# One list-scheduled order for attention and its filler products, with a shared pool of PSUM banks

## The chip, the core and the metric

The kernel runs on one core of one Trainium2 chip. The metric is the device time of one execution, in microseconds (us). The engines are TensorE (PE, matrix products), VectorE (DVE), ScalarE (ACT), GpSimd (POOL) and SyncE (SP, which issues the DMAs here).

## What is computed

```python
def _A_ref(x, wqkv, wo):                 # 32 heads of 16, 2048 tokens, D = 512
    q, k, v = split_heads(x @ wqkv)
    p = softmax((q @ k.T) * 16 ** -0.5)
    return merge_heads(p @ v) @ wo
def _B_ref(x, w_gate, w_up, w_down):     # F = 1792
    return ((x @ w_gate) * (x @ w_up)) @ w_down
xn = layernorm(x)
out = x + _A_ref(xn) * silu(_B_ref(xn))
```

All of it is float32. Products that need the accuracy are made as three products of high and low parts (`hi*hi + hi*lo + lo*hi`, each part in the float32r type).

## The kernel before

**Start.** `early` normalises the tokens, transposes them, and makes V and the first projections. It has PSUM banks of its own. It also makes the first 21 (`LEAD`) rounds of scores.

**Attention.** Work is cut into 32 units: 8 groups of four heads by 4 chunks of 512 queries. A unit has 16 key tiles of 128 keys. Each key tile takes, for each of the four heads `j`:

- a score `s` (`score`, L545, product at L550): queries by keys, from which DVE takes the maximum (L552). It runs 21 rounds ahead of where its unit is used. `maxima` (L554) gathers these, negates them and sends them through DRAM into extra rows of the query tile.
- a transposed score `t` (`expo`, L571, product at L575): keys by queries, with the negated maximum folded in by those extra rows. ACT takes the exponential (L577) into a tile `e`, of which there are 12.
- a V product (`pv`, L580, product at L586): V of the key tile, 32 columns a head, by `e`. The four heads stand side by side in the columns of the array and in one PSUM bank, summed over the 16 key tiles.

Heads with even `j` use the lower 64 rows of the array, odd ones the upper 64. So `t` of one head and `s` of another (`j ^ 1`) run at the same time, one on each half.

**Filler.** Everything else that PE has to do runs between these: projections of Q and K for later heads, then the gated product (gate `g`, up `u`, down `y`), then the output product (`z`). These sums are made in pairs of outputs by `pair` (L230): the sum of an output is split into the lower and the upper 64 rows of the operands. In the first half of a pair, output 0 takes its lower rows (L243) while output 1 takes its upper rows (L247); then the two change sides. Between the halves ACT reads one element of output 1 (`look`, L251), so that the second half waits until the first is in PSUM.

**Order.** The order of PE, ACT and DVE is the order in which the program issues instructions. The loop at L781 goes through 512 rounds, one key tile each: `t`, `s`, `t`, `s`, then a fixed share of the filler (`Filler.part`, 4 to 6 slots of two products), then `t`, `s`, `t`, `s`, then the V product of the round before. Copies and other work on ACT and DVE are put off by a fixed number of steps (`soon`, L99). PSUM's eight banks are divided by kind: two for `t`, three for `s`, one for `pv`, two for the filler (`BUFS`, L41). After the last round `finish` (L589) and `last_heads` (L503) close the last unit, and the last four heads are added to the last chunk of the output (`final`).

Of the kernel before, what the change touches and what calls it, by code (L numbers as in the profile page):

```python
# [32 lines left out]
FFN_ROUNDS = 484  # L33
SLOTS = 24 * (NC * (NG // 2 - 1) + 1) + 36 * NF * NC
SPLIT_ROUNDS = 4
EBUFS = 12
HBUFS = 2
FINAL_AT = 8
# [8 lines left out]
def body(ctx, tc, x, wqkv, wo, wg, wu, wd, out):  # L47
# [48 lines left out]

    steps, waiting = [0], []

    def soon(n, fn):  # L99

        if n:
            waiting.append((steps[0] + n, fn))
            waiting.sort(key=lambda w: w[0])
        else:
            fn()

    def flush():
        while waiting:
            waiting.pop(0)[1]()

    def step():
        steps[0] += 1
        while waiting and waiting[0][0] <= steps[0]:
            waiting.pop(0)[1]()

# [114 lines left out]
    def pair(outs, banks, sums, more=((), ()), stop=True):  # L230

        for k in range(2):
            low, high = [*more[k], *sums[k]], sums[1 - k]
            yield k, len(low)
            if k == 0:
                outs += [psum(tag, name) for tag, name in banks]
            for n in range(len(low)):  # L240
                m = n - len(low) + len(high)
                l, r = low[n]
                nc.tensor.matmul(outs[k], l[LOWER], r[LOWER], start=k == 0 and n == 0,  # L243
                                      stop=(stop or k == 0) and n == len(low) - 1, skip_group_check=k == 1)
                if m >= 0:
                    l, r = high[m]
                    nc.tensor.matmul(outs[1 - k], l[UPPER], r[UPPER], start=k == 0 and m == 0,  # L247
                                          stop=(stop or k == 0) and m == len(high) - 1, skip_group_check=k == 1)
                yield 1
            if k == 0:  # L250
                nc.scalar.activation(look, outs[1][0:1, 0:1], AF.Copy)  # L251


# [16 lines left out]

    def proj_pair(m, which):

        outs = []
        yield from pair(outs, [("misc", f"p{w}_{m}_{c}") for _, w, c in which],
                        [terms(lambda d: ws[0][:, d], lambda d: ws[1][:, d],
                               lambda d: xh[c][:, d], lambda d: xl[c][:, d], ND) for ws, _, c in which])
        raws = [qp.tile([P, D], F32, name="qr", bufs=3) for _ in outs]
        fst["high"] = nc.scalar.activation(raws[0], outs[0], AF.Copy)
        nc.vector.tensor_copy(raws[1], outs[1])
        for o, (_, w, c) in zip(raws, which):  # L280
            hl = qp.tile([P, 2, D], F32R, name="hl", bufs=HBUFS)
            split_rows(o, hl[:, 0], hl[:, 1])
            qk_store(hl, m, w, c)
# [19 lines left out]
    later = []  # L303

# [4 lines left out]
    def silu(fp, c, y):  # L309
        for t in range(4):  # L310
            e = fp.tile([P, D], F32, name="e2", bufs=1)
            nc.scalar.activation(e, y[:, t], AF.Tanh, scale=0.5)
            nc.gpsimd.tensor_scalar(e, e, 0.5, 0.5, op0=OP.mult, op1=OP.add)
            nc.gpsimd.tensor_tensor(y[:, t], e, y[:, t], op=OP.mult)
            if c < NC - 1:
                dma(YD[c][:, t], y[:, t])
            yield

    def gu_weights(f):
        fs = slice(f * P, (f + 1) * P)  # L320
        return [split(n, w[:, fs]) for n, w in (("w1", wg), ("w0", wu))]

    def ffn(nxt):
        fp = fst["fp"]
        for c in range(NC):
            if c == 0:
                fh, fl = xh[0], xl[0]
            else:
                fh, fl = [keep.tile([P, ND, 512], F32R, name=n) for n in ("fh", "fl")]
                dmar(fh, XD[c][0])  # L330
                dmar(fl, XD[c][1])
            y = fp.tile([P, 4, D], F32, name="y")
            for ti, fs in enumerate(THIRDS):
                hh = fp.tile([P, 5, 512], F32R, name="hh")
                hl = fp.tile([P, 5, 512], F32R, name="hl")
                dh = fp.tile([P, 5, D], F32R, name="dh")
                dl = fp.tile([P, 5, D], F32R, name="dl")
                for i, f in enumerate(fs):
                    ws = nxt
                    if not (c == NC - 1 and f == NF - 1):  # L340
                        nxt = gu_weights((f + 1) % NF)
                    outs = []
                    yield from pair(outs, [("misc", f"{n}{c}_{f}") for n in "gu"], [terms(lambda d: wh[:, d], lambda d: wl[:, d],
                                                 lambda d: fh[:, d], lambda d: fl[:, d], ND) for wh, wl in ws])
                    g = fp.tile([P, 512], F32, name="g", bufs=1)
                    nc.scalar.activation(g, outs[0], AF.Copy)
                    h = fp.tile([P, 512], F32, name="h", bufs=1)
                    soon(1, lambda h=h, u=outs[1], g=g: nc.vector.tensor_tensor(h, u, g, op=OP.mult))
                    soon(4, lambda h=h, hi=hh[:, i], lo=hl[:, i]: hidden(h, hi, lo))
                    raw = fp.tile([P, D], F32, name="wdr", bufs=2)  # L350
                    dma(raw, wd[f * P:(f + 1) * P])
                    nc.gpsimd.tensor_copy(dh[:, i], raw)  # L352
                    nc.gpsimd.tensor_tensor(dl[:, i], raw, dh[:, i], op=OP.subtract)
                if c == NC - 1 and fs[-1] == NF - 1:
                    fst["y"] = y
                    fst["w"] = [keep.tile([P, ND, D], F32R, name=n) for n in ("fh", "fl")]
# [4 lines left out]
                for t in range(0, 4, 2):  # L361
                    outs = []
                    yield from pair(outs, [("misc", f"y{c}_{ti}_{u}") for u in (t, t + 1)], [terms(lambda i: hh[:, i, u * P:(u + 1) * P],
                                                 lambda i: hl[:, i, u * P:(u + 1) * P],
                                                 lambda i: dh[:, i], lambda i: dl[:, i], len(fs)) for u in (t, t + 1)])
                    for n, o in enumerate(outs):
                        def add(o=o, y=y[:, t + n], first=ti == 0, n=n):
                            if first and n:
                                nc.vector.tensor_copy(y, o)
                            elif first:  # L370
                                nc.scalar.activation(y, o, AF.Copy)
                            else:
                                nc.vector.tensor_tensor(y, o, y, op=OP.add)
                        soon(n if ti else 0, add)
            later.append(silu(fp, c, y))

    ops = {}

    def o_split(c, tiles):
# [9 lines left out]
        ops[c] = now[0], tiles  # L391
# [5 lines left out]
    def prepare():  # L397

        done = [(NG - 1) * NC + c in finished for c in range(NC)]
        if 0 not in ops:  # L400
            if done[0] and "w" in fst:
                o_split(0, small_tiles())
        for c in (1, 2):
            if c not in ops and done[c] and ("big", c) in fst:
                h, l = fst["big", c]
                o_split(c, [(h[:, d], l[:, d]) for d in range(ND)])
        if 3 not in ops and "first" in fst:
            o_split(3, small_tiles())
# [18 lines left out]
    def ending():  # L427

# [6 lines left out]
        side = [big(n).bitcast(F32) for n in ("hh", "dl")]  # L435
        fst["big", 1] = big("hl"), big("dh")

        def until(c):
            while c not in ops or now[0] < ops[c][0] + SPLIT_ROUNDS:
                yield  # L440

        def chunk(c):
            yield from until(c)
            for t in range(0, 4, 2):
                here = side[t // 2]
                got = [(here[:, n], here[:, 2 + n]) for n in range(2)]

                def loads(t=t, here=here):
                    dma(here[:, 0:2], YD[c][:, t:t + 2])
                    dma(here[:, 2:4], x[(4 * c + t) * P:(4 * c + t + 2) * P].rearrange("(t p) d -> p t d", p=P))  # L450
                soon(2, loads)
                outs = []
                yield from pair(outs, [("misc", f"z{c}_{u}") for u in (t, t + 1)], [o_terms(c, u) for u in (t, t + 1)])
# [384 lines left out]
```

## Time and profile before

| | |
|---|---|
| median of 3 runs | 1816.97 us (1816.04 to 1818.2) |
| profiled execution, span from first to last instruction | 1815.7 us |
| PE busy | 1794.1 us (99%) |
| DVE busy | 1474.4 us (81%) |
| ACT busy | 1238.3 us (68%) |
| POOL busy | 580.7 us (32%) |
| DMA | 145.72 MB, mean 80 GB/s |
| mean granted clock of TensorE | 0.995 |

In a row of the profile, `L575 PE MATMUL t<-qs,ks` is an instruction of line 575 on PE that writes tile `t` and reads `qs` and `ks`; `x8` after it is the number of instructions merged into the row, and what stands in brackets is idle time of the engine before it and what ended it. Busy time of PE is the union of overlapping matmuls, whose ends are modelled: a busy PE is not yet a PE at its best rate. Better to read are the starts of its instructions.

### The profile page before, as it was taken

Reading aid. Unit: us, or ns where it says so; the run is one execution under the profiler, and the core shown is the slowest. Engines: PE = TensorE matmul, PEld = TensorE weight load, DVE = VectorE, ACT = ScalarE, POOL = GpSimd, SP = SyncE. Lnnn points to the kernel's source line nnn. Section 1 sums busy time; section 2 is a strip of 40 time slices with the busy share of each in tenths; the row PEclk is TensorE's granted clock in tenths of the full one; section 3 lists DMA queues with packets and bytes.
Section 4 is the critical chain, followed back from the end, with each engine's and each line's share of the span. In section 5 each row is a group of like instructions: output and inputs, shape, how many; then the busy total and the mean of one; then the engine's idle time right before and its main releaser. Section 6 shows DMA issues by size and latency. Waiting matters only on the chain.

```text
span 1815.7 us, 34194 instructions
## 1 busy us (share of the span) xinstructions
PE 1794.1 (99%) x13568; PEld 991.1 (55%) x13568; DVE 1474.4 (81%) x2456; ACT 1238.3 (68%) x2365; POOL 580.7 (32%) x647
## 2 busy tenths in 40 slices
PE   8899999999999999999999999999999999999998
PEld 5565555555555555555555555555555555555555
DVE  8488888888888888888888888888888888888832
ACT  5137676777776767777777777776767767767674
POOL 5321332431331325232132441431315323223441
PEclk9899999999999999999999999999999999999999
DMA  5424633520222122321115220411125111111352
GB/s 198 112 54 163 225 118 115 148 62 22 68 64 54 49 86 80 80 55 42 39 42 131 69 63 22 94 52 33 52 79 126 46 40 57 34 48 45 110 156 79
DMA packets 117227, 145.72 MB, mean 80 GB/s; under 512 B 12620, under 2 KB 74060, under 8 KB 114380
## 3 DMA queue, kind: packets, MB, share of 16 engines
q1 hardware_dynamic: 117068, 143.55, 27.7%
q8 instruction: 106, 1.74, 0.4%
q14 instruction: 53, 0.43, 0.1%
HBM read 95.94 MB, written 47.45 MB: 79 GB/s over the span
## 4 chain that ended last, share of the span: by engine, by line
PE 94%; DVE 2%; DMA 2%; POOL 1%; issue 0%; ACT 0%; SPq 0%; POOLq 0%; ACTq 0%; DVEq 0%
PE pv L586 27%; PE t L575 21%; PE s L550 11%; PE y L243 6%; PE u L243 5%; PE g L243 4%; PE u L247 4%; PE g L247 4%; PE y L247 3%; PE p L243 3%; PE v L224 2%; PE p L247 2%; PE z L243 1%; PE z L247 1%; DMA wdr<-in_wd_dram 1%; PE p L224 0%
## 5 line engine op out<-in xcount | busy, mean ns | idle before, releaser
L552 DVE TENSOR_REDUCE mx<-s 128x1 f32<-128x512 f32 x2048 | 1311.7, 683 | 268.5 <-PE s L550 162.7
L577 ACT ACTIVATE e<-t 128x512 f32<-128x512 f32 x2048 | 1111.9, 596 | 427.0 <-PE s L550 236.3
L550 PE MATMUL s<-ks,qs 48*128 48x512 f32 x2048 | 700.1, 427 | 10.0 <-DMA ks<-KD 8.8
L575 PE MATMUL t<-qs,ks 50*128 50x512 f32 x2048 | 705.2, 426 | 0.3 <-ACT e L577 0.3
L575 PEld LDWEIGHTS t<-qs,ks 50*128 50x128 f32 x2048 | 347.2, 185 | 499.4 <-ACT e L577 474.0
L586 PE MATMUL pv<-e,V 128*32 128x512 f32 x4096 | 545.7, 605 | 0.0
L550 PEld LDWEIGHTS s<-ks,qs 48*128 48x128 f32 x2048 | 337.4, 185 | 33.9 <-issue 12.9
L138 POOL CAST w0h<-w0r 128x512 fp32r<-128x512 f32 x60 | 36.7, 612 | 407.2 <-PE u L243 257.9
L586 PEld LDWEIGHTS pv<-e,V 128*32 128x32 f32 x4096 | 81.0, 108 | 156.5 <-issue 147.3
L352 POOL CAST dh<-wdr 128x512 fp32r<-128x512 f32 x56 | 33.8, 614 | 182.9 <-PE y L247 92.4
L247 PE MATMUL u<-fh,w0h 64*128 64x512 f32 x224 | 88.2, 394 | 0.1
L247 PE MATMUL y<-dh,hh 64*128 64x512 f32 x224 | 88.1, 393 | 0.0
L243 PE MATMUL u<-fh,w0l 64*128 64x512 f32 x224 | 88.0, 393 | 0.0
L243 PE MATMUL g<-fh,w1l 64*128 64x512 f32 x224 | 87.8, 392 | 0.0
L247 PE MATMUL g<-fl,w1h 64*128 64x512 f32 x224 | 87.8, 392 | 0.0
L243 PE MATMUL u<-fh,w0h 64*128 64x512 f32 x224 | 87.7, 392 | 0.0
L247 PE MATMUL g<-fh,w1h 64*128 64x512 f32 x224 | 87.7, 392 | 0.0
L243 PE MATMUL g<-fh,w1h 64*128 64x512 f32 x224 | 87.7, 391 | 0.0
L243 PE MATMUL u<-fl,w0h 64*128 64x512 f32 x224 | 87.6, 391 | 0.0
L243 PE MATMUL g<-fl,w1h 64*128 64x512 f32 x224 | 87.6, 391 | 0.0
L243 PE MATMUL y<-dh,hh 64*128 64x512 f32 x224 | 87.6, 391 | 0.0
L243 PE MATMUL y<-dl,hh 64*128 64x512 f32 x224 | 87.5, 391 | 0.0
(250 smaller groups left out, 2885.1 us busy)
## 6 DMA issues: line engine op xcount, KB each, us to landing
w1r<-in_wg_dram SPq DMA_DIRECT2D x56, 256.0 KB
w0r<-in_wu_dram SPq DMA_DIRECT2D x56, 256.0 KB
wdr<-in_wd_dram SPq DMA_DIRECT2D x56, 256.0 KB
qs<-QD SPq DMA_DIRECT2D x64, 192.0 KB
ks<-KD SPq DMA_DIRECT2D x12, 768.0 KB
KD<-hl SPq DMA_DIRECT2D x16, 512.0 KB
QD<-hl SPq DMA_DIRECT2D x16, 512.0 KB
OD<-tr SPq DMA_DIRECT2D x31, 256.0 KB
```

The source lines that it names most:

```text
L138: cast = nc.gpsimd.tensor_copy(hi, raw)
L224: nc.tensor.matmul(o, l(d), r(d), start=k == d == 0, stop=k == 2 and d == ND - 1)
L243: nc.tensor.matmul(outs[k], l[LOWER], r[LOWER], start=k == 0 and n == 0, stop=(stop or k == 0) and n == len(low) - 1, skip_group_check=k == 1)
L247: nc.tensor.matmul(outs[1 - k], l[UPPER], r[UPPER], start=k == 0 and m == 0, stop=(stop or k == 0) and m == len(high) - 1, skip_group_chec ...
L352: nc.gpsimd.tensor_copy(dh[:, i], raw)
L550: nc.tensor.matmul(o, QS[i][b:b + KB, pr, t * P:(t + 1) * P], k[b:b + KB, pr, kc * 512:(kc + 1) * 512], start=True, stop=True)
L552: nc.vector.tensor_reduce(MX[i][:, j, t, kc:kc + 1], o, axis=AX.X, op=OP.max)
L575: nc.tensor.matmul(o, k[b:b + KR, pr, kt * P:(kt + 1) * P], QS[i][b:b + KR, pr], start=True, stop=True)
L577: nc.scalar.activation(e, o, AF.Exp, scale=DH ** -0.5)
L586: nc.tensor.matmul(fst["pv"][32 * j:32 * j + 32], V[:, kt, h0:h0 + 32], es[j], start=kt == 0, stop=kt == NT - 1)
```

## The change

The loop of rounds, `Filler`, `pair`, `soon` and the steps go away. A list scheduler (`Order`) writes out the order of PE, ACT and DVE while the program is built. It keeps a clock for each of the three engines, with fixed costs of each kind of work as constants, and at each step picks what goes next on the two row halves.

- **Banks.** Seven PSUM banks form one pool that `t`, `s` and the filler share; one bank is left for `pv`. A bank comes free at a time that the scheduler works out.
- **Two rolling streams.** The filler is a sequence of single outputs (`Out`). Each has a lower part, made on the lower rows, then a look, then an upper part on the upper rows. The lower part of the next output and the upper part of the one before run at the same time, and a slot may also hold `t` or `s` beside a product of the filler. At most two outputs are held (`HELD`), a third if the upper one is in its last product.
- **V products.** A turn takes the V products of one or two key tiles of a unit. It waits for two while the filler is behind a pace of 4.95 slots (`PACE`) a key tile, and else for one.
- **Work on ACT and DVE** besides the exponentials and maxima is queued as tasks, which are placed when the engine is planned to be idle, or when they are urgent or late.
- **Some copies** change the engine: projections and the first third of `y` are now all copied by ACT. The weights of gate and up are loaded one at a time, and `h` has two buffers.

The core of the diff:

```diff
-BUFS = {"st": 2, "s": 3, "pv": 1, "misc": 2}
+POOL = 7
+PACE, PACE0 = 4.95, 0
+MOST = 4
+HELD, T_APART, S_APART, APART = 2, 3, 6, .4
+NEARLY, LEAN, AHEAD = 1, .1, 16
+SLOT, ENTER, TURN, LEAVE, AGAIN = .229, .105, .857, .10, .105
+T_SEEN, EXP_STEP, EXP_FREE, E_READY = .43, .494, .66, .65
+S_SEEN, MAX_STEP, MAX_FREE = .46, .609, .75
+ACT_AHEAD, DVE_AHEAD, ACT_FULL, DVE_FULL = .5, .9, .75, 1.2
...
+        def may_open(self):
+            return (self.low is None and self.next is not None
+                    and (self.held < HELD or self.held == HELD and self.nearly())
+                    and (self.next.ready is None or self.next.ready()))
+
+        def nearly(self):
+            o = self.high
+            return not self.mid[1:] and (o is None or len(o.terms[1]) - o.at[1] <= NEARLY)
+
+        def lean(self, x):
+            return LEAN * (AHEAD - (self.done[0] - self.done[1])) * (1 if x == 0 else -1)
...
+            if o.product(0):
+                self.low = None
+                self.mid.append(o)
+
+                def done(t, o=o):
+                    o.looked = t + LOOK_SEEN
+                self.task("act", self.pe + T_SEEN, LOOK, lambda: nc.scalar.activation(look, o.o[0:1, 0:1], AF.Copy),
+                          urgent=True, then=done)
...
+        def turn(self, ks):
+            for n in ks:
+                pv(n // 16, n % 16, self.es.pop(n))
+                del self.eready[n]
+            self.turns += len(ks)
+            self.pe += ENTER + TURN * len(ks) + LEAVE
+            self.after = True
+            if self.turns % 16 == 0:
+                heads(self, self.turns // 16 - 1)
...
+            temit, semit = sum(self.tpos), sum(self.spos) - 4 * LEAD
+            nf = self.banks() - (1 if self.may_open() else 0)
+            full = temit - 4 * self.turns > EBUFS - 1
+            lead = semit - temit
...
+            t_ok = bool(tx) and nf > 0 and not full and (lead > -3 or s_over) and len(self.tout) < MOST
+            s_ok = bool(sx) and nf > 0 and lead < 5 and len(self.sout) < MOST
+            batch = 2 if self.turns % 16 < 15 and sum(self.done) / 2 < PACE * self.turns + PACE0 else 1
+            if temit - 4 * self.turns < 4 * batch:
+                if self.act - self.pe > ACT_AHEAD:
+                    t_ok = False
+                if self.dve - self.pe > DVE_AHEAD:
+                    s_ok = False
...
+            ks = []
+            while len(ks) < (2 if self.turns % 16 < 15 else 1):
+                k = self.turns + len(ks)
+                if len(self.es.get(k, ())) < 4 or self.eready[k] > self.pe:
+                    break
+                ks.append(k)
+            ready = len(ks) >= batch
+            last = min(self.tpos) >= 2 * NU * 16
+            if ready and (full or last or self.act - self.pe >= ACT_FULL and (self.dve - self.pe >= DVE_FULL or s_over)) and not (t_ok or s_ok):
+                return self.turn(ks)
...
+            if ops is None:
+                ops = {x: "f" for x in (0, 1) if can[x]}
+                if len(ops) < 2 and ready:
+                    return self.turn(ks)
+                if not ops:
+                    return self.wake()
...
-        ctx.enter_context(banks_of(BUFS))
-        for n in range(NU * 16):
...
+        fst["banks"] = ctx.enter_context(tc.tile_pool(name="banks", bufs=1, space=PSUM, reuse_waits="tile"))
+        order_ = Order(outs(wq0))
+        todo = list(range(4))
+        while not order_.over():
+            order_.step()
```

More of the change, by code (lines that the diff above doesn't have):

```diff
@@ L433, in big, with first @@
             return fp.tile([P, 5, 512], F32R, name=n)
[L435 to L448, printed above, removed]
+        def first():
+            fst["side"] = [big(n).bitcast(F32) for n in ("hh", "dl")]
+            fst["big", 1] = big("hl"), big("dh")
@@ L490, in ending, with evac, one @@
[L490 to L501 removed]
+                    sides[t // 2] = 2
+            def evac(ready, gone):
+                here = fst["side"][t // 2]
+                def one():
+                    end(c, t, o.o, here[:, t % 2], here[:, 2 + t % 2])
+                    sides[t // 2] -= 1
+                order_.task("dve", ready, PRODUCT, one, then=gone)
@@ L821, in body @@
+        for t in todo:
+            final(t)
     ffp.close()
```

782 lines of the change are left out of this document (501 added, 281 removed).

## Prediction

> **What bounds the kernel now.** I read the page's totals and chain first, then its groups.
>
> ```profile
> span 1815.7 us, 34194 instructions
> PE 1794.1 (99%) x13568; PEld 991.1 (55%) x13568; DVE 1474.4 (81%) x2456; ACT 1238.3 (68%) x2365; POOL 580.7 (32%) x647
> ...
> PE 94%; DVE 2%; DMA 2%; POOL 1%; issue 0%; ACT 0%; SPq 0%; POOLq 0%; ACTq 0%; DVEq 0%
> ...
> L552 DVE TENSOR_REDUCE mx<-s 128x1 f32<-128x512 f32 x2048 | 1311.7, 683 | 268.5 <-PE s L550 162.7
> L577 ACT ACTIVATE e<-t 128x512 f32<-128x512 f32 x2048 | 1111.9, 596 | 427.0 <-PE s L550 236.3
> ```
>
> 94% of the chain is PE; DVE and ACT wait for PE (268.5 and 427.0 us idle before their two main groups). So the time is the sum of what PE issues. One turn of the loop shows what that costs; this is the timeline of PE alone, start and length in us:
>
> ```profile
> 903.75 1.07 PE L586 MATMUL pv<-e,V 128*32 128x512 f32 x8
> 904.75 0.49 PE L575 MATMUL t<-qs,ks 50*128 50x512 f32 x1
> ...
> 905.09 0.39 PE L575 MATMUL t<-qs,ks 50*128 50x512 f32 x1
> 905.31 0.39 PE L243 MATMUL y<-dl,hh 64*128 64x512 f32 x1
> ...
> 906.48 0.39 PE L575 MATMUL t<-qs,ks 50*128 50x512 f32 x1
> ...
> 906.72 0.39 PE L575 MATMUL t<-qs,ks 50*128 50x512 f32 x1
> 907.04 1.07 PE L586 MATMUL pv<-e,V 128*32 128x512 f32 x8
> ```
>
> A slot carries two matmuls, one on each half of the rows. The five product slots from 905.31 to 906.48 cost 1.17, so 0.233 each. A V product (pv) holds PE 1.00 until the next pair; the pair behind it takes 0.34 instead of 0.233 (0.11 more), and the last pair before it 0.32 (0.09 more). A V product of one key tile thus costs 1.20. Nine slots and one V product are 9 x 0.233 + 1.20 = 3.30; the rows show 907.04 - 903.75 = 3.29. PE does not wait here: it switches.
>
> ```profile
> L586 PE MATMUL pv<-e,V x4096: 592/593/618, 122.3 to 1800.1; 128*32 128x512 f32 x196
> ...
> 1798.46 2.25 PE L586 MATMUL pv<-e,V 128*32 128x512 f32 x16
> ...
> 1799.67 0.14 PEld L586 LDWEIGHTS pv<-e,V 128*32 128x32 f32 x2 [0.20 <-ACT e L577]
> 1800.64 0.49 PE L243 MATMUL z<-fh,w0h 64*128 64x512 f32 x1
> ```
>
> The loop over 512 key tiles begins its V products at 122.3; the 511th begins at 1798.46 (the last two run back to back). That is 1676.2 / 510 = 3.287 a tile. From the code: four t and four s make 4 slots a tile; the 202 outputs of the filler (26 projections, 112 gate and up, 48 down, 16 last) are 5028 half-row products, 2514 slots, 4.91 a tile. 8.91 x 0.233 + 1.20 = 3.276. What is left for waits is 0.011 a tile, 6 us in all. A better order alone has nearly nothing to win; only the switches have, 512 x (1.20 less what the V product itself streams).
>
> **The change part by part.** *V products of two key tiles in one turn.* The price of a second tile lies in the one place where two stand together, the end of the loop, taken there pass by pass:
>
> ```profile
> 1798.91 0.61 PE L586 MATMUL pv<-e,V 128*32 128x512 f32 x4
> ...
> 1799.34 0.61 PE L586 MATMUL pv<-e,V 128*32 128x512 f32 x3
> ```
>
> A tile is two passes of four matmuls; a pass follows the one before, from the first tile into the second, after 0.43. A second tile is 0.86, a merged turn 1.20 + 0.86 = 2.06 against 2.40: 0.34 saved. From below: the whole batch of sixteen took 2.18 until the next product (1798.46 to 1800.64), and 2.18 + 0.20 for both switches saves only 0.02. But that batch waited for the last exponential (weights at 1799.67, 0.33 behind the pass of 1799.34), so I take 0.34 and keep 0.02 as the bound. [...]
>
> Units have 16 tiles, so at most 256 merges: 87 us. How many can be had depends on DVE, which PE cannot feed during a turn:
>
> ```profile
> 600.00:900.00 300.00, 300.00 (x2348) 162.94 (x2348) 255.56 (x421) 216.89 (x415) 94.80 (x104) 1.00 0.23 61
> ...
> 600.00:900.00 300.00, 236.59 (x378) 1.00 0.23 61
> ...
> 599.72 0.72 PE L550 MATMUL s<-ks,qs 48*128 48x512 f32 x2
> ...
> 600.28 2.69 DVE L552 TENSOR_REDUCE mx<-s 128x1 f32<-128x512 f32 x4 [0.37 <-PE s L550]
> ...
> 609.08 1.28 DVE L552 TENSOR_REDUCE mx<-s 128x1 f32<-128x512 f32 x2
> ```
>
> Columns of the first row, from 600 to 900 us: PE, PE loads, DVE, ACT, POOL, clock, DMA; the second row is DVE on the maxima alone. 255.56 us of DVE to 378 maxima is 5.41 for the eight of two tiles. ACT's 216.89 is less, so DVE decides. Two tiles with a merged turn take 17.82 x 0.233 + 2.06 = 6.21, so DVE may idle 0.80. From the start of the batch PE is away 1.00 + 0.86, and a score is seen 0.56 after its start (599.72 to 600.28): 2.42 in which DVE lives on queued scores, 0.60 each (1.28 - 0.683). Three queued leave 0.62 idle, which fits; two leave 1.22, which does not. Seven shared banks, two held by products, leave five: three s and two t. When a third product bank is held there are four, two and two.
>
> With two queued, a merged period is 5.41 + 1.22 = 6.63; PE fills it with (6.63 - 2.06 - 1.86) / 0.233 = 11.6 product slots, more than the 9.82 there are, and the pace rule (4.95 a tile) then asks for single turns. Singles idle DVE 1.56 - 1.20 = 0.36, so two last 2 x (2.70 + 0.36) = 6.12 with 8.0 product slots. A share a of merged tiles balances at 11.6a + 8.0(1 - a) = 9.82, a = 0.5: 44 us. With three queued a is 1: 87. I have nothing in the trace to choose by, since before gives each kind its own banks, and take the middle: 65 us, about 190 merges, on PE and so on the path.
>
> *Two rolling streams.* Before, two outputs go up and down together and hardly a half is alone. Now the upper half of an output waits for its look, and a new lower half opens only while no more than two outputs are held, or the upper one is in its last product. A lone product costs a slot as a pair does:
>
> ```profile
> 1804.51 0.67 PE z L243 x3
> ...
> L251 ACT ACTIVATE look<-u x56: 144/160/163, 335.7 to 1665.1; 1x1 f32<-1x1 f32 x56
> ```
>
> The three of the chain take 0.22 each, so half of a slot, 0.117, is lost. None need be lost, since a t or s can stand beside it; three at each of 202 outputs would lose 71 us. I take one at every second output, 101 x 0.117 = 12 us, nearer the lower end because t and s are free to change sides.
>
> *More looks, copies moved to ACT.* There is now one look an output instead of one for two, some 101 more of 0.160: 16 us on ACT. In-order ACT waits there for PE's last lower product, with exponentials queued behind. Thirteen projection copies and eight of y go from DVE to ACT, at ACT's 0.596 each, 13 us. Both lie in ACT's 427 us of idle time: nothing. Without that cover it would be 29 us. DVE gets lighter by as much.
>
> *Loads.* Weights come singly, one output of the same kind ahead, so 24 slots, 24 / 4.91 x 3.2 = 16 us. SP and POOL carry the same transfers and casts; POOL is busy 94.80 of 300. Nothing; were one load in ten late by 1 us, 11 us for the 112.
>
> *Bank waits and the order itself.* The list scheduler removes up to the 6 us of waits in the loop; its fixed costs can bring as many back where they miss. Zero, between -6 and +30 (0.06 a tile). *Start and close.* What comes ahead of the loop is issued by the same code. The chain behind the last V product, 1798.46 to 1815.7, keeps its transposes and last products: nothing, within 5.
>
> Sum: 1815.7 - 65 + 12 = 1763. The lone products of the close (the row at 1804.51) are now paired or gone earlier, which I put at 4: 1759. The profile's span is 1.3 under the median 1816.97, so 1760.
>
> **The rivals.** *Starved maxima, slower.* After each merged turn DVE has fewer scores than it needs, and the products cannot fill because their own evacuations stand in the same queues: g's copy behind exponentials, h's product behind maxima, y behind the split of h. It decides once DVE idles over 2 x 3.287 - 5.41 = 1.16 a merged turn, so with two scores queued or fewer. At two: (6.63 - 6.57) x 256 = 15 us more, with one lone half at each output 24 more: 1856. For it: DVE at 85% (255.56 of 300). Against it: both engines wait for PE today, and a turn can wait until the queues are filled. [...]
>
> *The merges do not happen.* Products run ahead of the pace and a quarter of the pairs merge: 64 x 0.34 = 22 us less, lone halves 18 more: 1813, no change. For it: the batch is two only while the products lag behind 4.95 a tile, and they average 4.91.
>
> *Everything merges.* Three scores are always queued, no half is alone: 1817 - 87 - 4 = 1726. For it: 0.62 of idle fits into 0.80.
>
> **How the numbers follow.** Forecast 0.56; starved 0.13; not merged 0.14; all merged 0.17. About 0.2% is what a measurement of this kernel can tell from no change. Faster takes the forecast, all merged and 0.08 of the not merged: 0.81; same 0.04; slower 0.15. The range goes from a little under all merged, 1718, to the not merged, 1812; it leaves out the starved case and some of the not merged one.
>
> **What would show it.** Right: PE still over 97% busy and the chain PE's; pv in groups of sixteen for about three pairs of tiles in four, 1.86 from the first pv to the next t; the slot still 0.233; DVE near 89% of the loop with idle time of 0.6 to 1.2 behind merged turns. Wrong: groups of eight nearly everywhere (pace); PE idle before t, s or u with maxima or exponentials named (starved); many slots with one matmul (streams); a second tile dearer than 0.92.

## The result: 1829.33 us, and the profile after

| | before | after |
|---|---|---|
| median of 4 runs each | 1817.26 us (1816.04 to 1818.2) | 1829.33 us (1826.38 to 1834.84) |
| ratio after / before, 95% interval | | 1.007 [1.005, 1.009] |
| profiled execution | 1815.7 us span | 1832.05 us, 1830.3 us span |

The change makes the kernel slower by 0.7%. The forecast was 1760 with a range of 1718 to 1812.

The totals, the chain by engine and the three main groups of after (busy us, mean ns of one; then idle time before the group and what ended most of it):

```profile
span 1830.3 us, 34996 instructions
PE 1797.4 (98%) x13568; PEld 1057.7 (58%) x13568; DVE 1433.9 (78%) x2433; ACT 1238.7 (68%) x2487; POOL 588.8 (32%) x649
...
PE 92%; DMA 3%; DVE 2%; POOL 1%; ACT 1%; issue 0%; SPq 0%; ACTq 0%; POOLq 0%; DVEq 0%
...
L943 DVE TENSOR_REDUCE mx<-b 128x1 f32<-128x512 f32 x1964 | 1232.8, 683 | 287.7 <-PE b L941 136.9
L971 ACT ACTIVATE e<-b 128x512 f32<-128x512 f32 x2048 | 1109.4, 600 | 475.4 <-PE b L969 242.2
...
L980 PE MATMUL pv<-e,V 128*32 128x512 f32 x4096 | 515.2, 605 | 0.2 <-DVE tr L1007 0.2
```

By this page little has happened: PE is still 98% busy and 92% of the chain. But PE's busy time has gone up by 3.3 us for the same 13568 matmuls, and with fewer switches it should have come down by some sixty. A busy share near 100% hides both what was won and what was lost; the starts of PE's instructions show it. PE alone around a merged turn of after, start and length in us:

```profile
605.54 0.40 PE L288 MATMUL b<-fh,w1l 64*128 64x512 f32 x1
605.59 0.39 PE L288 MATMUL b<-fh,w0l 64*128 64x512 f32 x1
605.91 1.92 PE L980 MATMUL pv<-e,V 128*32 128x512 f32 x16
607.76 0.49 PE L941 MATMUL b<-ks,qs 48*128 48x512 f32 x1
...
608.10 0.39 PE L969 MATMUL b<-qs,ks 50*128 50x512 f32 x1
...
608.33 0.39 PE L969 MATMUL b<-qs,ks 50*128 50x512 f32 x1
```

The last slot ahead of the turn takes 605.91 - 605.59 = 0.32, the two V products 607.76 - 605.91 = 1.85, the slot behind 0.34, the next again 0.23. All of it is as the prediction priced it (1.86 for the turn). So the merge does what it should, and the time is lost elsewhere.

**Where the time went.** I divided PE's time from the first `t` (at 116 us in both) to its last product, slot by slot, from the starts in the trace: 0.1165 for each half-row product (1054 us in all) and 0.858 for each V product tile (439 us) are work. Of the rest, up to 0.092 ahead of a turn, 0.138 at its end and 0.105 behind it are the switch; 0.1165 for a slot with one product is a lone half; everything else is a wait, the time lost at a lower clock included.

| us of PE | before | after | difference | predicted |
|---|---|---|---|---|
| turns of two / of one | 1 / 510 | 171 / 170 | | 190 merged |
| switches | 169 | 113 | -56 | -65 |
| lone halves | 9 | 34 | +24 | +12 |
| waits | 22 | 68 | +47 | 0 (-6 to +30) |
| sum | | | +15 | |

The sum is the difference of the spans, 14.6. Nearly as many merges came as predicted; the lone halves cost twice as much; the waits took the rest of the gain, more than the top of their bound.

**What the waits are.** Gaps of over 0.06 make up 56 of the 68 us. By what ended them: maxima 11.3 us in 74 gaps, the query rows back from DRAM 6.7 in five, exponentials 5.5 in 34, the low part of h from POOL 3.0 in four, looks 2.6 in seven; 24.2 us in 216 gaps have no releaser, most of them about 0.105 long; a V product at half clock counts here too. Many of the gaps without a releaser are waits after all, of the weight loads and not of the products. One of them, weight loads (PEld) and products:

```profile
202.18 0.18 PEld L941 LDWEIGHTS b<-ks,qs 48*128 48x128 f32 x1 [0.26 <-ACT e L971]
...
202.19 0.49 PE L941 MATMUL b<-ks,qs 48*128 48x512 f32 x1
202.20 0.48 PE L969 MATMUL b<-qs,ks 50*128 50x512 f32 x1
...
202.52 0.40 PE L288 MATMUL b<-fl,w0h 64*128 64x512 f32 x1
```

The load for an `s` waited for an exponential (in the shared pool its bank may have held a `t`) and began at 202.18, with its product at 202.19. PE did not stand still, but the slot took 202.52 - 202.19 = 0.33. Of 87 full slots of this length with no wait to be seen ahead of them, 81 have a load that began within 0.03 us of its product, and in 61 of the 87 the load had waited for an exponential; of 3058 slots of the usual length only 88 have so late a load.

**Where the waits are.** I counted the waits and the lone halves by unit, from the first V product of a unit to that of the next (slots paired by starts less than 0.15 apart, which gives 24 and 67 us of waits in place of 22 and 68):

| | before | after | kept_pace (below) |
|---|---|---|---|
| waits, units 0 to 27 (us) | 18 | 45 | 37 |
| waits, units 28 to 30 (us) | 3 | 20 | 7 |
| lone halves, units 0 to 27 | 16 | 166 | 137 |
| lone halves, units 28 to 30 | 6 | 81 | 70 |

So more than half of what is lost is spread over the units in which the filler lasts: 27 us of waits, and 150 lone halves, 17 us. The end of the filler, units 28 to 30, takes 17 and 9 us.

Three places show how the longer waits come about. First the one long kind, in the chain of after (start, length):

```profile
526.27 1.85 PE pv L980 x16
...
528.63 2.03 DVE mx L943 x4
...
531.86 1.94 DMA MD<-mt
...
534.11 6.78 DMA qs<-MD
...
541.02 0.46 PE b L969
```

The last maxima of a chunk go through DRAM: 1.94 out and 6.78 back. `t` of the next chunk waits for them at 541.02, and PE stands still for 2.25 us (in brackets at the right of the same product in the timeline):

```profile
541.02 0.46 PE L969 MATMUL b<-qs,ks 50*128 50x512 f32 x1 [2.25 <-DMA qs<-MD]
...
541.33 0.39 PE L941 MATMUL b<-ks,qs 48*128 48x512 f32 x1
```

The slot behind the wait takes 541.33 - 541.02 = 0.31, where 0.233 is usual. What follows costs more. Stretches of 3.4 us of after (columns: length, PE, PE loads, DVE, ACT, POOL, granted clock, DMA, GB/s):

```profile
538.30:541.70 3.40, 1.15 (x11) 0.78 (x8) 1.07 (x2) 0.12 (x1) 0.00 (x0) 1.00 1.06 172
541.80:545.20 3.40, 3.40 (x17) 3.01 (x16) 1.93 (x3) 2.70 (x7) 0.00 (x0) 0.50 0.99 136
1402.00:1405.40 3.40, 3.40 (x18) 1.65 (x12) 1.41 (x2) 1.83 (x5) 0.00 (x0) 0.50 0.97 149
...
1739.90:1743.30 3.40, 3.40 (x20) 1.01 (x14) 0.77 (x3) 0.15 (x1) 3.32 (x4) 0.50 0.08 11
```

Behind the wait the clock is granted at 0.50 for the next 3.4 us: PE is "busy" all through, with 17 matmuls where some 27 are usual (before has 1804 in the 230 us from 1500 on). There are six such stretches in the loop of after, 24 us in all and so 12 us lost; the loop of before has none. How many there are differs from run to run: the four runs of after have mean clocks of 0.993, 0.991, 0.988 and 0.987 at 1826.38, 1826.61, 1832.05 and 1834.84 us, and the profiled one is the third of these. The last of the six has no DMA wait in front. It is in the units where the filler has run out. The products of the filler alone in three units of after (a unit is 16 key tiles; the row's count is its matmuls, the first columns are PE, PE loads, clock):

```profile
1511.80:1565.30 53.50, 32.66 (x167) 22.36 (x167) 1.00 0.10 29
1615.60:1667.60 52.00, 21.46 (x90) 12.71 (x89) 0.97 0.16 46
1667.60:1721.50 53.90, 17.95 (x79) 12.13 (x79) 0.91 0.16 56
```

Unit 26 has 167 of them, units 28 and 29 have 90 and 79. In its first 28 units after uses 5.10 slots of filler a tile, where before used 4.83 and the pace asks for 4.95; the last outputs `z` open only when a chunk's last heads are done, at the end of unit 28. Units 28 to 30 then have 44, 40 and 52 slots (before 76, 76 and 96), and about 20 us of waits in the three, where the 28 units ahead have 1.6 us each on average (before 0.6). Without filler PE has only `t`, `s` and V products left, and the timeline of after shows its rate there:

```profile
1737.72 0.49 PE L941 MATMUL b<-ks,qs 48*128 48x512 f32 x1
1738.32 0.49 PE L969 MATMUL b<-qs,ks 50*128 50x512 f32 x1
...
1738.92 0.50 PE L969 MATMUL b<-qs,ks 50*128 50x512 f32 x1
1739.35 3.18 PE L980 MATMUL pv<-e,V 128*32 128x512 f32 x16
1742.46 0.80 PE L941 MATMUL b<-ks,qs 48*128 48x512 f32 x2
```

Slots 0.60 apart instead of 0.233, which is the spacing of the maxima (seven in 4.28 us from 1736.38 on, at 0.683 each, so 0.60 apart; seven exponentials in 3.58, so 0.50 apart), and then a turn of 3.11 instead of 1.85, with the clock at 0.50 (last row of the stretches above).

### The profile page after: what moved, and what is told of

Same layout as the page of the kernel before. It is cut to its first block, busy times and chain, and to the rows that moved or that the text cites. A ratio compares the mean times of both kernels' runs of the same rounds, so it can differ in the third digit from the quotient of the medians.

```text
span 1830.3 us, 34996 instructions
## 1 busy us (share of the span) xinstructions
PE 1797.4 (98%) x13568; PEld 1057.7 (58%) x13568; DVE 1433.9 (78%) x2433; ACT 1238.7 (68%) x2487; POOL 588.8 (32%) x649
## 3 DMA queue, kind: packets, MB, share of 16 engines
q1 hardware_dynamic: 117068, 143.55, 27.3%
## 4 chain that ended last, share of the span: by engine, by line
PE 92%; DMA 3%; DVE 2%; POOL 1%; ACT 1%; issue 0%; SPq 0%; ACTq 0%; POOLq 0%; DVEq 0%
PE b L288 32%; PE pv L980 26%; PE b L969 16%; PE b L941 15%; PE v L211 2%; DVE mx L943 1%; DMA qs<-MD 1%; PE p L211 1%; PE s L941 1%; DMA MD<-mt 0%; DMA ks<-KD 0%; ACT e L971 0%; DMA wdr<-in_wd_dram 0%; DMA qs<-QD 0%; DMA ks<-in_x_dram 0%
## 5 line engine op out<-in xcount | busy, mean ns | idle before, releaser
L943 DVE TENSOR_REDUCE mx<-b 128x1 f32<-128x512 f32 x1964 | 1232.8, 683 | 287.7 <-PE b L941 136.9
L971 ACT ACTIVATE e<-b 128x512 f32<-128x512 f32 x2048 | 1109.4, 600 | 475.4 <-PE b L969 242.2
L969 PE MATMUL b<-qs,ks 50*128 50x512 f32 x2048 | 776.3, 418 | 7.6 <-DMA qs<-MD 6.0
L941 PE MATMUL b<-ks,qs 48*128 48x512 f32 x1964 | 758.5, 424 | 0.7 <-DVE mx L943 0.3
L969 PEld LDWEIGHTS b<-qs,ks 50*128 50x128 f32 x2048 | 366.4, 186 | 173.0 <-DVE mx L943 47.3
L941 PEld LDWEIGHTS b<-ks,qs 48*128 48x128 f32 x1964 | 338.8, 186 | 197.2 <-ACT e L971 66.4
L288 PE MATMUL b<-fh,w1h 64*128 64x512 f32 x504 | 201.0, 402 | 0.6 <-ACT look L385 0.3
L288 PE MATMUL b<-fh,w0h 64*128 64x512 f32 x500 | 199.1, 400 | 0.0
L288 PE MATMUL b<-fh,w1l 64*128 64x512 f32 x504 | 198.4, 398 | 0.0
L288 PE MATMUL b<-fl,w1h 64*128 64x512 f32 x504 | 197.8, 396 | 0.0
```

Of the source, the lines that this page charges most:

```text
L288: nc.tensor.matmul(self.o, l[rows], r[rows], start=x == 0 and n == 0, stop=last and (x == 0 or not self.kept), skip_group_check=x == 1)
L941: nc.tensor.matmul(o, QS[i][b:b + KB, pr, t * P:(t + 1) * P], k[b:b + KB, pr, kc * 512:(kc + 1) * 512], start=True, stop=True)
L943: nc.vector.tensor_reduce(MX[i][:, j, t, kc:kc + 1], o, axis=AX.X, op=OP.max)
L969: nc.tensor.matmul(o, k[b:b + KR, pr, kt * P:(kt + 1) * P], QS[i][b:b + KR, pr], start=True, stop=True)
L971: nc.scalar.activation(e, o, AF.Exp, scale=DH ** -0.5)
```

## The experiments

The theory that I tested: the merge is worth what was predicted, and the new order gives it back in waits, because merged turns let the filler run ahead and run out and leave maxima late. The rivals: the merge itself is worth less (the price of the batch of sixteen); the maxima on DVE are the bound, whatever the order; or the new order costs this with or without merges. The medians beside before, whose own median in these jobs is 1816.1 to 1816.5, and the division of PE's time as above:

| kernel | us | ratio [95%] | turns of two / one | switches | lone | waits | us at half clock |
|---|---|---|---|---|---|---|---|
| single_turns | 1889.5 | 1.0404 [1.0388, 1.0419] | 0 / 512 | 171 | 24 | 78 | 44 |
| hand_merged | 1921.47 | 1.0577 [1.0561, 1.0592] | 256 / 0 | 85 | 19 | 197 | 10 |
| hand_merged_two | 1979.71 | one run | 256 / 0 | 85 | 7 | 272 | 0 |
| six_banks | 1955.07 | one run | 123 / 266 | 130 | 39 | 169 | 82 |
| half_maxima | 1819.54 | 1.0013 [1.0003, 1.0023] | 171 / 170 | 113 | 32 | 60 | 10 |
| slack_plan | 1837.29 | 1.0114 [1.0099, 1.0129] | 147 / 218 | 121 | 36 | 62 | 31 |
| kept_pace | 1821.19 | 1.0029 [1.0016, 1.0042] | 132 / 248 | 127 | 28 | 49 | 0 |
| early_maxima | 1840.72 | 1.0134 [1.0119, 1.0149] | 174 / 164 | 113 | 32 | 81 | 44 |
| pace_head | 1816.21 | 1.0000 [0.9991, 1.0010] | 120 / 272 | 131 | 24 | 44 | 3 |
| pace_nearly | 1825.02 | 1.0047 [1.0035, 1.0060] | 95 / 322 | 139 | 19 | 49 | 7 |
| pace_start | 1824.73 | 1.0049 [1.0035, 1.0062] | 120 / 272 | 131 | 25 | 51 | 7 |

### single_turns: the new order without merges

```diff
-            batch = 2 if self.turns % 16 < 15 and sum(self.done) / 2 < PACE * self.turns + PACE0 else 1
+            batch = 1
...
-            while len(ks) < (2 if self.turns % 16 < 15 else 1):
+            while len(ks) < 1:
```

> The changed kernel with one key tile in every turn (512 turns in place of 341). Theory A (a merge is worth 0.34 us of PE and nothing else; the change lost elsewhere, in the small waits and lone halves of the scheduled order): switching rises by 171 x 0.34 = 58 us, waits stay near 68 us in the loop, so about 1885 us. Theory B (the merges starve DVE and ACT and bring the waits on themselves): the waits fall back to near the 21 us of the kernel before and lone halves fall too, so about 1835 to 1845 us.

Measured 1889.5: 60 us over after for 171 merges, 0.35 each. The division gives 58 of it to the switches, 0.34 each; waits are up by 10 and lone halves down by 10. So the second price of the prediction, 0.02, is out. Theory A came out, also for the waits: without a single merge they are 78 us, not 21, so they do not need the merge. But the row is also 73 us over before, at the same number of turns: the order as this scheduler makes it is dearer than the one by hand where every turn is single. Its loop ends early, with 554 slots of the filler left behind it:

```profile
L980 PE MATMUL pv<-e,V x4096: 592/616/1064, 120.2 to 1722.6; 128*32 128x512 f32 x196
```

The last V product starts at 1722.6, about 166 us before the end. So this kernel also moves filler out of the loop (3.9 slots a tile in its first 28 units), and its 73 us are not the price of the order alone: 14 us of its waits and 140 of its 212 lone halves lie behind the loop, and its 44 us at half clock make up 22 of the waits.

### hand_merged and hand_merged_two: merges in the order by hand

Both are before, with its own banks for each kind, and with the V products of two key tiles in one turn, every second round. hand_merged_two has this alone; hand_merged also puts filler at one more place in every second round, so that more of it stands around the turn.

```diff
-            if prev is not None:
-                pv(*prev)
+            if len(kept_back) == 2:
+                for prev in kept_back:
+                    pv(*prev)
+                kept_back = []
+            kept_back.append((i, kt, es))
...
-FFN_ROUNDS = 484
+FFN_ROUNDS = 726
...
-                if j == 1:
+                if j == 1 or j == 3 and n % 2:
...
-                        fil = Filler(ending(), lambda n: 2)
+                        fil = Filler(ending(), lambda n: 3)
```

The last three edits are hand_merged's alone: they add the place and fit the filler's shares to it.

> The kernel before with its hand-written order and its own banks for each kind, but with the V products of two key tiles in every second round, and the filler in three parts to two rounds. Theory A: 256 merges x 0.34 = 87 us less, about 1730 us, up to 1745 with a few waits. Theory B (a turn of two starves DVE and ACT): at least 1800 us, with t and s waiting for maxima and exponentials behind the turns.

> hand_merged with the filler where the kernel before has it, in one part to each round, so that between two merged turns four slots of t and s stand together. If the waits of hand_merged (197 us) come from its own banks for each kind, two of them for t: the third and fourth t of each such four wait for exponentials, about 1 us a merge, 256 us and more: 1950 us or above. If they come only from where hand_merged put the filler: below 1850 us.

Measured 1921.47 and 1979.71, although all 256 merges are there and the switches cost 85 instead of 169. Waits eat it: 197 and 272 us. `t` on PE, the turn and ACT in hand_merged_two, from one merged turn on:

```profile
1586.27 1.92 PE L586 MATMUL pv<-e,V 128*32 128x512 f32 x16
...
1588.12 0.49 PE L575 MATMUL t<-qs,ks 50*128 50x512 f32 x1
...
1588.46 0.39 PE L575 MATMUL t<-qs,ks 50*128 50x512 f32 x1
...
1588.65 1.09 ACT L577 ACTIVATE e<-t 128x512 f32<-128x512 f32 x2 [1.42 <-PE s L550]
...
1589.85 0.40 PE L575 MATMUL t<-qs,ks 50*128 50x512 f32 x1
...
1590.09 0.39 PE L575 MATMUL t<-qs,ks 50*128 50x512 f32 x1
...
1591.27 0.50 PE L575 MATMUL t<-qs,ks 50*128 50x512 f32 x1 [0.78 <-ACT e L577]
...
1591.76 0.50 PE L575 MATMUL t<-qs,ks 50*128 50x512 f32 x1
```

ACT stands idle for 1.42 us over the turn, but the `t` right behind the turn do not wait. The wait comes at the fifth `t` (0.78 in brackets): four `t` of two rounds follow each other here, from 1589.85 on, with neither filler nor a turn between them, and `t` has two banks. The third of the four has to wait for an exponential, as was expected, and the order being fixed, PE stands with it; in 245 of the 256 periods a wait is at this fifth `t`. In hand_merged filler stands between these rounds; its waits are at `t` as well and at the filler's own banks (the products of h, the sums of y and the copies of g). So merging costs 105 us (hand_merged) and 163 us (hand_merged_two) in orders by hand that are not fitted to it, and merging with a shared pool of banks and a planned order costs 12. What merging costs in a hand-made order that is fitted to it was not measured, nor was the shared pool without the planned order.

### six_banks: one bank less in the pool

```diff
-POOL = 7
+POOL = 6
```

> The changed kernel with six banks in the pool in place of seven, everything else as it is. If banks are what merges, pairs and waits hang on: 123 merges in place of 171 (16 us), some 640 lone halves in place of 290 (40 us), and waits up by 40 us or more: 1920 us or more. If banks are not scarce: under 1850 us.

Measured 1955.07: 126 us over after for one bank in seven, with 101 us more of waits and 82 us at half clock. The 123 merges came as expected, the lone halves not (39 us, some 340 and not 640). Products of the filler alone in units 20, 23 and 27 of six_banks:

```profile
1321.70:1381.00 59.30, 41.63 (x216) 28.83 (x215) 1.00 0.31 65
1485.90:1537.50 51.60, 0.00 (x0) 0.00 (x0) 0.90 0.24 42
1681.90:1729.80 47.90, 0.00 (x0) 0.00 (x0) 0.93 0.05 15
```

Most of it is again a filler that has run out. In its first 21 units the kernel uses 6.7 slots of filler a tile, with fewer merges than after, and then has none in seven whole units, 22 to 28. Of the 101 us of new waits 88 lie in units 21 to 30, and 9 in the first 21 (41 against 32). In the code PE takes filler whenever no `t` or `s` may be placed, and nothing holds the filler back: `PACE` only chooses the size of a turn. With a bank less `t` and `s` can be placed less often. What the seventh bank would be worth with a filler that lasts was not measured.

### half_maxima: are the maxima the bound?

```diff
-        nc.vector.tensor_reduce(MX[i][:, j, t, kc:kc + 1], o, axis=AX.X, op=OP.max)
+        nc.vector.tensor_reduce(MX[i][:, j, t, kc:kc + 1], o[:, 0:256], axis=AX.X, op=OP.max)
...
-        nc.scalar.activation(e, o, AF.Exp, scale=DH ** -0.5)
+        nc.scalar.activation(e, o, AF.Exp, scale=.01 * DH ** -0.5)
```

> The changed kernel in the same order, but each maximum is taken over 256 of its 512 columns (the exponentials are scaled down so that they stay finite; the softmax is not the reference's). DVE's main work gets about a third shorter and the banks of s come free earlier, while PE, ACT and all counts of turns and lone halves stay. If PE's waits in the loop come from scores' banks and from maxima that are late, 20 to 30 us of the 68 go: near 1803 us. If DVE does not hold PE up: within 5 us of 1829.

The order of issue stays that of after. The group of the maxima in half_maxima:

```profile
L943 DVE TENSOR_REDUCE mx<-b 128x1 f32<-128x256 f32 x1964 | 787.1, 421 | 694.3 <-PE b L941 399.6 <-PE b L969 137.3 <-PE b L288 127.3
```

A maximum takes 421 instead of 683 ns, which relieves DVE of 446 us. The time falls by 10 us, with waits from 68 to 60 and the half clock from 24 us to 10. So of the 47 us of new waits some 8 hang on DVE's speed, and the clock has 7 of these. They lie in units 28 to 30 (20 us of waits before, 12 now); in the first 28 units the waits stay at 44. In this order, then, the speed of the maxima is a small part of the cause. But the order is still the one that was planned for the slow maxima, with its filler running out at the same place: what an order planned for faster maxima would gain was not measured.

### slack_plan: constants nearer to what the chip takes

```diff
-SLOT, ENTER, TURN, LEAVE, AGAIN = .229, .105, .857, .10, .105
-T_SEEN, EXP_STEP, EXP_FREE, E_READY = .43, .494, .66, .65
-S_SEEN, MAX_STEP, MAX_FREE = .46, .609, .75
+SLOT, ENTER, TURN, LEAVE, AGAIN = .233, .10, .858, .14, .105
+T_SEEN, EXP_STEP, EXP_FREE, E_READY = .46, .50, .75, .72
+S_SEEN, MAX_STEP, MAX_FREE = .49, .615, .85
```

> The changed kernel with the scheduler's constants nearer to what the chip shows: slot 0.233, turn 0.14 to leave, banks of t free 0.75 and of s 0.85 after their reader begins, results seen 0.03 later. If PE's small waits come from a plan that hands out banks too early: 20 us less of waits in the loop for 24 merges fewer (8 us), near 1817 us. If the waits have nothing to do with the plan's constants: 1837 us or more.

Measured 1837.29, 8 us over after: waits 62 instead of 68, but 24 merges fewer (switches +8) and 31 us at half clock. That is what was expected if the constants are not the reason. A later estimate of every bank buys few waits and pays for them in merges.

### kept_pace: merges only while the filler is behind

In after `batch` says how many tiles a turn waits for, but a turn takes two whenever two are ready. Here it takes no more than `batch`.

```diff
-            while len(ks) < (2 if self.turns % 16 < 15 else 1):
+            while len(ks) < batch:
```

> The changed kernel, but a turn takes no more key tiles than the pace rule asks for, so that the filler cannot run ahead: it lasts until unit 29 in place of unit 28. If the waits and lone halves of the last five units (24 and 14 us) come from the filler having run out there, they fall by about 25 us together; about 40 merges are lost, 13 us: near 1817 us. If they have another cause: near 1842 us.

Measured 1821.19, 8 us less than after with 39 merges fewer. The switches cost 13 more, the lone halves 6 less, the waits 19 less, with no stretch at half clock (12 less in all; the two profiled executions are 11 apart), and units 28 to 30 have 72, 76 and 50 slots of filler. It came out nearer to the 1817 of the theory than to 1842. Of the waits that go, 12 us are those of units 28 to 30, and with them the five half-clock windows that after has there. This is the plainest run for that part of the theory: merges beyond the pace are paid for at the end of the filler. It is also its limit: in the first 28 units 37 us of waits stay, twice those of before.

### early_maxima, pace_head, pace_nearly, pace_start: the lateness and the pace

early_maxima sends a chunk's maxima off earlier and lets `t` of the next chunk be planned later. pace_head is that together with kept_pace and a pace of 4.85 with a head start of 20 slots. pace_nearly and pace_start are pace_head with one more edit each: a third output may open sooner, and a slower pace with a longer head start.

```diff
-MAXIMA, MAXIMA_WAIT, REST, KNOWN = .45, 4.0, .15, 6.0
+MAXIMA, MAXIMA_WAIT, REST, KNOWN = .45, 1.0, .15, 10.0
...
-PACE, PACE0 = 4.95, 0
+PACE, PACE0 = 4.85, 20
...
-NEARLY, LEAN, AHEAD = 1, .1, 16
+NEARLY, LEAN, AHEAD = 6, .1, 16
...
-PACE, PACE0 = 4.85, 20
+PACE, PACE0 = 4.8, 30
```

> The changed kernel, but the second part of a unit's maxima is planned 1 us after the first in place of 4, and their way through DRAM at 10 us in place of 6. If PE's longest single waits (five of up to 2.4 us, 6.7 in all, for the query tile's maxima rows) come from a plan that counts on them too early, they go, with the small waits behind them: 8 us less, near 1821 us. If the landing itself is late whatever the plan: 1829 us.

> kept_pace with the pace at 4.85 slots and a head start of 20, and the maxima planned as in early_maxima: about 120 merges. Against kept_pace (1821 us): 12 merges fewer (4 us), some 50 lone halves fewer (6 us), DMA waits and the waits of the last units down by 5 us: near 1814 us, level with the kernel before. If the waits are the same whatever the pace: 1825 us.

> pace_head, but a third output may be opened once the upper one has six products left, in place of one: 166 lone halves in place of 218 in the order (6 us less), 95 merges in place of 120 (8 us more), waits about 2 us less: 1816 us. If the third bank takes more from t and s than the order counts: 1825 us or more.

> pace_head with the pace at 4.8 slots and a head start of 30: the same 120 merges and 222 lone halves, so the filler lasts a little longer: 1814 us if the last units' waits still cost something, 1816 us if not.

early_maxima missed: 1840.72, 11 us over after. The waits for the query rows do go, from 6.7 us to 0.2. But the order moves, and the filler runs out sooner. Filler products alone in units 27 to 29 of early_maxima (PE, PE loads, clock):

```profile
1564.80:1624.10 59.30, 19.69 (x87) 11.87 (x87) 0.93 0.22 70
1624.10:1671.90 47.80, 0.00 (x0) 0.00 (x0) 0.86 0.06 18
1671.90:1728.30 56.40, 20.56 (x92) 13.81 (x92) 0.86 0.13 44
```

The second stretch has none at all and a mean clock of 0.86. The long wait in the chain was real, and the end of the filler cost more than it. The same units of pace_head:

```profile
1549.50:1600.30 50.80, 30.70 (x145) 21.12 (x144) 1.00 0.12 35
1600.30:1652.30 52.00, 32.50 (x158) 22.28 (x157) 1.00 0.19 50
1652.30:1708.40 56.10, 34.30 (x153) 22.31 (x152) 1.00 0.26 81
```

145 to 158 products in each, clock 1.00. Its 1816.21 is 13 us under after and level with before; it is the best version of the new order that I found, and none is faster than before. Against before its 120 merges save 39 us of switches, and 15 us of lone halves and 22 of waits take nearly all of it back. pace_nearly removes lone halves (24 to 19) and loses 25 merges and 5 us of waits for them; pace_start keeps the 120 merges and has 7 us more of waits. pace_start missed, and of the two ends named for pace_nearly the second came, 1825: neither is faster than pace_head.

## Why the prediction was wrong

- **What bounds the kernel.** Right: the chain is PE's, the slot is 0.233 and a switch 0.34, and a better order had little to win. The 6 us of waits are too few: the sum put all 2048 `s` and all 2514 slots of filler into the loop, but 84 `s` (42 slots) are made ahead of it by `early` and 21 slots behind it, 15 us together. By the starts before has 22 us of waits.
- **V products of two key tiles in one turn.** Right in mechanism and price: 1.85 for a turn of two (predicted 1.86), 0.35 a merge over all of single_turns against after (predicted 0.34, with 0.02 as the other bound). The switch is paid once a turn, of one tile or of two: 169 us over the 511 turns of before, 171 over the 512 of single_turns, 113 over the 341 of after and 85 over the 256 of hand_merged are 0.33 each. Mis-sized: 171 merges instead of 190, so 56 us instead of 65. That the count came so near is luck. The prediction took the middle between two and three queued scores; the trace of after shows the case of two. From 200 to 1500 us DVE is idle for 1.24 us on average in the 2.92 us from the start of a merged turn, and for 0.40 in the 2.06 from that of a single one, where the prediction had 1.22 and 0.36 for two. By its own rates for that case (11.6 and 8.0 product slots for two tiles) the filler feeds 128 merges to the end, not 190. After made 171 and used the filler up early; kept_pace, which keeps to the pace, makes 132.
- **Two rolling streams.** Mis-sized: 287 lone halves instead of 101, 34 us by the starts of after, 24 more than before and not 12.
- **Bank waits and the order itself: "Zero, between -6 and +30".** This is the step that failed. It measured +47. I argued from before that PE nowhere waits, and so gave the new order none. Two things stand in its place. First, the planned order itself: 27 us of the new waits lie in units 0 to 27, where the filler lasts, some 7 of them with the query rows that came late and the half clock behind them. Waits like these stay without merges (60 us in the same units of single_turns), and 37 of the 45 us there stay with the pace kept. The part of them that I could follow is weight loads that wait for a bank, mostly for an exponential. Second, the end of the filler: 17 us in units 28 to 30. Before has filler in a fixed share to the end, while in the new order each merged turn takes filler ahead to cover itself. The rate that I worked out myself for a merged period, 11.6 slots for two tiles against 9.82 there are, says this. I drew from it only that the pace rule would then ask for single turns. The code does not: the rule sets what a turn waits for, and a turn takes two anyway. kept_pace closes that gap and gives 8 us back with fewer merges.
- **The clock.** No term at all. 24 us at 0.50 are 12 of the 47 us in the profiled run. Before has 0.995 as its mean clock and no such stretch in its loop. Its start has them, though: the clock is 0.50 from 51.7 to 61.9 us, behind 6.80 us in which PE was busy for 2.61, and from 75.6 to 79.0, behind 3.50 us with 1.93. So its trace did show stretches with little PE work that were followed by 10.2 and 3.4 us at half clock.
- **"Starved maxima, slower."** Right sign, 1856 against 1829, and two of its terms came: DVE idles 1.24 us a merged turn, over its 1.16, and the lone halves cost 24 us more. But it said that PE would lack work behind each merged turn. The filler covers that as long as there is any, and with DVE relieved of 446 us in the same order the kernel gains 10, in the last units, where filler is lacking first.
- **More looks, loads, start and close.** Looks ended 2.6 us of gaps. The close is not 4 us shorter but 5 longer: 39 slots remain behind the loop of after, in 20.1 us, against 15.1 before.
- **What would show it.** Of the signs named, PE over 97% busy, 1.86 for a turn and the slot at 0.233 came out right and yet the kernel is slower. "Three pairs of tiles in four" should have been two in three (171 of 256). DVE did not come nearer to its limit, 89% of the loop: its share of the span fell from 81% to 78%, and its idle time before the 2048 maxima rose from 268.5 to 318 us (287.7 before the 1964 of the loop and 30.0 before the 84 of the start).

What stays open: how much of the remaining waits of pace_head, 44 us against 22, is the pool of banks and how much the looks and the order of copies; whether 256 merges can be had with the filler lasting to the end; what the small waits of the first 28 units would take to go, which none of the runs removed; and, for the gaps without a releaser that are not late weight loads, what set each of them off. More than 12 tiles `e` were not tried, nor a larger pool: its seven banks and the one for `pv` are the eight that before uses too.

## What to carry to other kernels

A saving per turn is a saving only if the work that fills the longer turn lasts to the end: count the filler by stage, in units of the loop, and not as a mean over the whole, and let the order hold it back. A planned order has a price of its own, here 27 us of waits and 17 us of lone halves while the filler lasted. When a bottleneck engine is busy 98% before and after, divide its time from the starts of its instructions into work, switches, lone halves and waits; the busy share shows none of these. Merging in the order by hand, and the pool with the planned order but without merges, were each far slower than the whole change, which itself is slower than before.

## What the runs showed of the hardware

- In the loop of after the granted clock falls to 0.50 for 3.41 us, once for twice that (6.83 us from 1668.2 on), and then returns. In before it does so at the start, for 10.24 us from 51.7 and for 3.41 from 75.6. The six stretches of after begin at 541.8, 1402.0, 1627.2, 1668.2, 1695.5 and 1739.9; the distances, 860.2, 225.2, 41.0, 27.3 and 44.4 us, are within 0.1 whole multiples (252, 66, 12, 8 and 13) of 3.4133, a third of the 10.24. The first stretch came behind a wait of 2.25 us, in 3.40 us of which PE was busy 1.15; the last came behind slots 0.60 apart, without a long wait. In the 3.41 us ahead of the six PE issued 0.20, 0.26, 0.47, 0.59, 0.61 and 0.59 of what it could (slots at 0.233, V products at 0.858); the windows from 804.6, 623.7 and 1685.3 on, with 0.52, 0.59 and 0.67, were followed by a full clock, so no sharp threshold can be read off.
- In after, slots whose weight load had to wait took about 0.1 more than the usual 0.233: 0.31 at 541.02 and 0.33 at 202.19 above, much as a slot behind a switch (0.34). A wait for a bank can so cost 0.1 us although PE shows no idle time (81 of the 87 slots counted above).
